# Attention and a two-layer MLP on one core: weight sums moved from GpSimd to VectorE, activation tables fetched by tiny activations, scores and sums rescheduled

## The chip, the cores and the metric

The kernel runs on one core of a Trainium2 chip. The metric is device time in microseconds (us), median over runs. TensorE (PE) multiplies, VectorE (DVE), ScalarE (ACT) and GpSimd (POOL) do the rest, and the DMA engines, 16 on the profile's page, move data. Every time in this text comes from a timed run or from the profile of one execution. Such an execution is some 2 us shorter in its span than in its time, as the span runs from the first to the last of the program's own instructions. An execution is called slow here when its time is more than 1.5% above the fastest of the same kernel, and fast otherwise; ratios are of fast runs alone.

## The reference

```python
# q, k, v: (8 batches, 8 heads, 576 tokens, 64)
q_c, k_c, v_c = (t.reshape(B, H, 9, 64, 64) for t in (q, k, v))      # chunks of 64 tokens
scores = q_c @ k_c.transpose(0, 1, 2, 4, 3) / sqrt(64)
attn = softmax(scores)                                               # within a chunk
x = (attn @ v_c) -> (4608 tokens, 512)                               # heads side by side
h = x @ w_in                                                         # 512 x 2048
g = h * sigmoid(beta * h)
out = g @ w_out                                                      # 2048 x 512
```

## The kernel before

The 4608 tokens are nine blocks of 512 (0 to 8). A block goes through layer 1 (`h`, Silu) and layer 2 (`out`), while the attention of a later block is fitted in between: transposes of q and k on VectorE (`T_items`), scores on PE and exponentials on ScalarE (`emit_sc`), the attention product on PE and its norm on VectorE (`emit_pv`), and a transposing DMA into `xt`. Blocks 1 to 8 use a Strassen-Winograd scheme with seven products in place of eight. It needs sums of weights (`sw`, and `tw` for layer 2), of activations (`xs`) and of Silu outputs (`s1` to `s4`). In the traces an engine's instructions come in the order in which the program emits them: in the changed kernel the last copy to `xt` starts at 56.63 us, behind the table load of 55.23 to 56.51 that is emitted ahead of it.

The weight sums of layer 2, four operations of 128 x 2048 elements:

```python
    def emit_tw(n):
        ...
        o, a_, b_ = {1: (t1, b12, b11), 2: (t2, b22, t1), 3: (t3, b22, b12), 4: (t4, b21, t2)}[n]
        nc.gpsimd.tensor_tensor(out=o, in0=a_, in1=b_, op=ALU.subtract)
```

Half of layer 1 (`unit`; `prod` is four matmuls, `snap` a copy from PSUM on VectorE, a spacer is one plain tile of layer 1, and more):

```python
        prod("A", a11, b11, True)
        snap("u1", "A")
        prod("B", a12, b21, True)
        nc.vector.tensor_tensor(out=c1[:, :, up_], in0=bank["B"], in1=sb["u1"], op=ALU.add)
        spacers[0]()
        prod("A", swr[1], ts[1], False)       # the first one to need xs, and u1 copied
        ...
        for i in range(2):
            silu(m2 + i, up_, bank["A"][:, i])
        for i in range(2):
            silu(m2 + i, dn_, sb["t"][:, i])
        for i in range(2):
            silu(m1 + i, slice(0, BLK), c1[:, i])
```

Norm and transpose of one attention product (`x16` comes from a pool of three buffers):

```python
            nc.vector.reciprocal(out=rr, in_=xx[:, :, :, D:D + 1])
            nc.vector.tensor_tensor(out=yy, in0=src, in1=rr.to_broadcast(shape), op=ALU.mult)
        ...
            nc.sync.dma_start_transpose(out=xt_t[j][:, :, t0:t0 + 128], in_=xf)
```

Layer 2 of block j, from block 2 on (`mm` are the seven products of 16 matmuls, `pv` is the attention product with its norm, `fill` holds eight sums `s1` and `s2`):

```python
            mm[0](); emit_sum(j, 3, 1); emit_sum(j, 3, 3)
            pv(0)
            dve(4)                      # four of the sums
            mm[1](); cB(); pv(1)
            while fill: dve()           # the other four
            mm[2](); pv(2)
            mm[3](); pv(3); sc(0)
            emit_sum(j, 4, 0); emit_sum(j, 4, 1)
            mm[4](); emit_sum(j, 4, 2); emit_sum(j, 4, 3); cD()
            mm[5](); cC(); sc(1); emit_xs(na); mm[6]()
```

Block 1 computes four groups of scores (for blocks 2 and 3) and from there on the kernel is one block ahead.

The softmax here doesn't subtract the row's maximum and nothing guards it: scores larger than these inputs give would overflow.

## Time and profile before

| | before |
|---|---|
| time | 321.67 us median of 3 runs (320.79 to 321.75) |
| span of the profiled run | 318.4 us |
| PE busy | 274.9 us, 86% |
| mean granted clock of PE | 0.984 |

From the page of the kernel before, the PE line of the busy times and the line of the clock, in tenths for 40 slices of the span (PEld is TensorE's loading of weights, x the number of instructions):

```profile
PE 274.9 (86%) x3520; PEld 191.0 (60%) x3520; DVE 227.8 (72%) x411; ACT 159.2 (50%) x270; POOL 119.4 (38%) x114
PEclk9999999789989999999999999999999999999999
```

PE is the engine to keep busy; two places show a lower clock. The timeline tells where PE stood idle. Its columns are start and duration in us, engine, line, operation, tiles written and read, number of instructions, and in brackets the idle time before and what ended it. Four stretches of PE in the kernel before:

```profile
54.32 1.03 PE L244 MATMUL hps<-xt,wi 128*128 128x512 f16 x4
62.19 1.01 PE L297 MATMUL wA<-xs,sw 128*128 128x256 f16 x4 [6.84 <-DVE u L305]
...
89.36 0.45 PE L158 MATMUL sc<-qT,kT 32*64 32x64 f16 x32 [0.47 <-DVE kT L130]
93.62 0.32 PE L158 MATMUL sc<-qT,kT 32*64 32x64 f16 x8 [3.81 <-DVE kT L130]
...
209.70 0.28 PE L397 MATMUL oA<-w_out,gt 128*128 128x256 f16 x1 [0.67 <-ACT gt L308]
210.31 1.38 PE L397 MATMUL oA<-w_out,gt 128*128 128x256 f16 x11 [0.33 <-ACT gt L308]
...
219.39 0.32 PE L186 MATMUL x<-vb,et 64*64 64x65 f16 x16 [1.21 <-DVE x L203]
```

The first pair is the start of block 1: the product that needs `u1` copied and `xs` waits 6.84 us for VectorE. The second is layer 2 of block 1: scores wait 3.81 us for a key transpose. The last three lines are from block 5 and return in other blocks: 1.0 us at the start of layer 2 for Silus, and 1.21 us in front of the fourth attention product for the norm of the third.

Why VectorE is late at 55 us: its timeline and that of GpSimd, in the kernel before.

```profile
44.69 3.13 DVE L121 TENSOR_SCALAR w_out<-w_out,binv 128x512 f16<-128x512 f16 x4 [2.58 <-DMA w_out<-in_moe_w_out_dram]
...
54.27 2.42 DVE L277 TENSOR_TENSOR xs<-xt 128x512 f16<-128x512 f16 x1 [0.17 <-ACT xt L223]
56.72 4.15 DVE L278 TENSOR_TENSOR xs<-xt,xs 128x512 f16<-128x512 f16 x1
60.79 0.41 DVE L279 TENSOR_TENSOR xs<-xt 128x512 f16<-128x512 f16 x1
```

```profile
48.19 8.22 POOL L369 TENSOR_TENSOR tw<-w_out,tw 128x2048 f16<-128x2048 f16 x2
56.35 4.24 POOL L369 TENSOR_TENSOR tw<-w_out 128x2048 f16<-128x2048 f16 x1
```

Operations of the same shape take 0.41 us or 2.42 and 4.15 us; the two long ones end at 56.69 and 60.87, and GpSimd's sums end at 56.41 and 60.59.

The clock around the two holes, from the view of stretches (from:to, length, then per engine the busy time and the number of instructions in the order PE, PEld, DVE, ACT, POOL, then the granted clock, the DMA share and GB/s):

```profile
62.20:64.00 1.80, 1.80 (x9) 1.31 (x9) 1.38 (x2) 0.00 (x0) 0.00 (x0) 0.50 0.00 0
64.00:66.00 2.00, 2.00 (x9) 0.82 (x8) 1.85 (x2) 0.20 (x1) 0.00 (x0) 0.56 0.04 8
...
93.60:97.00 3.40, 3.38 (x26) 2.52 (x27) 0.00 (x0) 1.08 (x2) 0.00 (x0) 0.57 0.00 0
```

The clock was 0.50 from 58.95 to 65.78 us and from 93.08 to 96.50, that is until 3.6 us after the end of the first hole and 2.9 us after that of the second. In the first stretch four matmuls of 128x512 took 1.91 us (from 63.85), and just behind it 1.03 (from 66.11), so these two holes cost more than their length.

One more line, from VectorE's timeline of block 2: the last norm of a block waits for a DMA.

```profile
125.87 0.69 DVE L203 TENSOR_TENSOR x<-x,rd 128x512 f16<-128x512 f32 x1 [0.56 <-DMA xt<-x]
```

Its `x16` buffer is that of the first norm of the block (three buffers), whose transposing DMA was issued at 118.33 and had landed only at 125.78. The median on the page for such transposes is 3.0 us, and one in block 5, where no q and k batch is loaded, took 2.4 (213.01 to 215.41). In between ran the loads of a q and a k batch, issued at 115.60 and 116.33, landed at 121.08 and 125.33. In blocks 3 and 4 the first transpose landed 0.4 us after the load of k as well (157.27 after 156.82, 188.90 after 188.48).

### The profile page before, as it was taken

The page shows a single profiled execution, that of the slowest core. Times are in us where ns is not written, and L with a number is a line of the kernel's source. Part 1 is how long each engine was busy: PE and PEld are TensorE (multiplying, and loading weights), DVE is VectorE, ACT ScalarE, POOL GpSimd, SP SyncE. Part 2 cuts the span into 40 slices and gives each one's busy share as a digit, 9 for nine tenths or more (in the row PEclk, how much of TensorE's full clock was granted, in tenths as well). Part 3 has the DMA queues.
Part 4 walks back from the last instruction along what each step waited for, and adds up shares of the span by engine and source line. Part 5 has one row for each costly group of instructions (what it writes and reads, how often), then busy time and mean ns, then how long its engine had stood idle before and what let it go on. Part 6 is the DMA issues. An engine that isn't in the chain of part 4 may idle for free.

```text
span 318.4 us, 8248 instructions
## 1 busy us (share of the span) xinstructions
PE 274.9 (86%) x3520; PEld 191.0 (60%) x3520; DVE 227.8 (72%) x411; ACT 159.2 (50%) x270; POOL 119.4 (38%) x114
## 2 busy tenths in 40 slices
PE   2889988198949988998899889988998899889894
PEld 0464444155836656766675667666766676676583
DVE  3673467977875878787878786878756775686574
ACT  1268244267423852585257535753584458415820
POOL 8633299616104261346133614341443113213400
PEclk9999999789989999999999999999999999999999
DMA  7999999600933939393949393904390430152002
GB/s 116 179 208 212 187 210 200 173 2 6 191 90 73 70 45 190 106 87 51 184 115 77 56 182 115 74 19 85 103 73 19 84 101 1 30 83 90 2 33 99
DMA packets 69588, 31.99 MB, mean 100 GB/s; under 512 B 53680, under 2 KB 63920, under 8 KB 69552
## 3 DMA queue, kind: packets, MB, share of 16 engines
q0 software_dynamic: 44960, 18.35, 47.9%
q1 hardware_dynamic: 24448, 12.99, 17.4%
q8 instruction: 27, 0.44, 0.6%
q10 hardware_dynamic: 144, 0.13, 0.1%
q14 instruction: 9, 0.07, 0.1%
HBM read 36.71 MB, written 9.44 MB: 145 GB/s over the span
## 4 chain that ended last, share of the span: by engine, by line
PE 43%; DVE 29%; DMA 12%; ACT 9%; issue 5%; POOL 1%; DVEq 0%; ACTq 0%; POOLq 0%
PE oA L397 12%; PE hps L244 11%; DMA w_out<-in_moe_w_out_dram 10%; ACT gt L308 7%; PE wA L297 6%; DVE x L203 5%; DVE s L357 5%; PE wX L297 5%; PE oC L397 4%; DVE s L355 3%; DVE kT L130 3%; PE sc L158 3%; DVE qT L130 2%; DMA ku<-in_k_dram 2%; DVE osb L416 2%
## 5 line engine op out<-in xcount | busy, mean ns | idle before, releaser
L244 PE MATMUL hps<-xt,wi 128*128 128x512 f16 (+1 forms) x336 | 81.2, 372 | 0.8 <-ACT xt L223 0.7
L254 ACT ACTIVATE gt<-hps,beta 128x512 f16<-128x512 f32 x80 | 52.6, 684 | 25.9 <-PE hps L244 25.7
L397 PEld LDWEIGHTS <-s 128*128 128x128 f16 x496 | 47.5, 99 | 7.0 <-DVE s L361 0.3
L244 PEld LDWEIGHTS <-wi 128*128 128x128 f16 x336 | 33.0, 98 | 23.8 <-issue 1.6
L397 PEld LDWEIGHTS <-gt 128*128 128x128 f16 x384 | 35.8, 98 | 16.1 <-ACT gt L308 10.2
L305 DVE COPY u<-wA 128x512 f32<-128x512 f32 x48 | 33.0, 688 | 16.7 <-PE wA L297 16.7
L397 PE MATMUL oA<-tw,s 128*128 128x256 f16 x368 | 44.1, 273 | 0.0
L328 POOL TENSOR_TENSOR t<-u,w 128x512 f32<-128x512 f32 x16 | 20.6, 1285 | 55.8 <-PE hps L244 36.5
L297 PEld LDWEIGHTS <-sw 128*128 128x128 f16 x256 | 25.4, 99 | 19.4 <-issue 9.8
L408 ACT COPY u<-oA 128x512 f32<-128x512 f32 x24 | 14.1, 588 | 43.5 <-PE oA L397 43.5
L466 POOL TENSOR_TENSOR o<-t,o 128x512 f32<-128x512 f32 x7 | 8.9, 1267 | 66.6 <-ACT o L463 66.6
L98 POOL DMA_DIRECT2D vb<-in_v_dram x32 | 27.4, 875 | 10.1 <-DMA wi<-in_moe_w_in_dram 6.3
L167 ACT ACTIVATE et<-sc 128x512 f16<-128x512 f32 x34 | 18.5, 594 | 24.6 <-PE sc L158 24.4
L297 PE MATMUL wA<-xs,sw 128*128 128x256 f16 x128 | 19.7, 278 | 6.8 <-DVE u L305 6.8
L203 DVE TENSOR_TENSOR x<-x,rd 128x512 f16<-128x512 f32 x34 | 23.5, 691 | 2.7 <-DMA xt<-x 1.7
L435 POOL TENSOR_TENSOR w<-u,u 128x512 f32<-128x512 f32 x7 | 10.2, 1458 | 39.6 <-ACT u L408 34.2
L297 PEld LDWEIGHTS <-wi 128*128 128x128 f16 x192 | 18.7, 98 | 9.8 <-issue 4.4
L130 DVE STREAM_TRANSPOSE qT<-qu 128x576 f32<-128x576 f32 x16 | 20.0, 1250 | 5.7 <-DMA qu<-in_q_dram 5.5
L158 PE MATMUL sc<-qT,kT 32*64 32x64 f16 x1088 | 14.1, 196 | 11.4 <-DVE kT L130 11.1
L397 PE MATMUL oA<-w_out,gt 128*128 128x256 f16 x128 | 17.7, 274 | 7.0 <-ACT gt L308 7.0
L167 ACT ACT_TABLE_LOAD x7 | 9.0, 1283 | 28.8 <-PE sc L158 28.8
L158 PEld LDWEIGHTS <-kT 32*64 32x64 f16 x1152 | 12.2, 111 | 16.3 <-DVE kT L130 12.5
(83 smaller groups left out, 444.2 us busy)
## 6 DMA issues: line engine op xcount, KB each, us to landing
out_dram<-osb SPq DMA_DIRECT2D x21, 256.0 KB, 2.7
vb<-in_v_dram POOLq DMA_DIRECT2D x32, 144.0 KB, 5.5
qu<-in_q_dram POOLq DMA_DIRECT2D x7, 576.0 KB, 6.5
ku<-in_k_dram POOLq DMA_DIRECT2D x7, 576.0 KB, 10.0
out_dram<-o SPq DMA_DIRECT2D x14, 256.0 KB, 2.2
wi<-in_moe_w_in_dram POOLq DMA_DIRECT2D x4, 512.0 KB, 12.5
w_out<-in_moe_w_out_dram POOLq DMA_DIRECT2D x4, 512.0 KB, 16.8
qu<-in_q_dram POOLq DMA_DIRECT2D x2, 288.0 KB, 5.4
```

The costliest lines, as they stand in the source:

```text
L98: nc.gpsimd.dma_start(out=t[64 * hp:64 * hp + 64, 2 * z:2 * z + 2, :, 0:D].rearrange("p s c d -> p (s c) d"), in_=v[b, h0:h0 + 2].rearrang ...
L130: nc.vector.transpose(out=dst[b][:, z].rearrange("p t r e -> p (t r e)").bitcast(FP32).rearrange("p (t r) -> p r t", r=RUN), in_=src[b][:, ...
L158: nc.tensor.matmul(out=sc[a % 2][o0:o0 + 64, z, c, :], lhsT=kk[:, cb * CH:(cb + 1) * CH, e], rhs=qq[:, cb * CH:(cb + 1) * CH, e], start=(e ...
L167: nc.scalar.activation(out=et, in_=sc[s], func=ACTF.Exp, scale=scale)
L203: nc.vector.tensor_tensor(out=yy, in0=src, in1=rr.to_broadcast(shape), op=ALU.mult,)
L244: nc.tensor.matmul(out=hps_t[j, m][:, c0:c1], lhsT=w_r[m // 4][:, 2 * z + e, m // 2 % 2, m % 2, :], rhs=xt_t[j][:, n, c0:c1], start=(n == ...
L254: nc.scalar.activation(out=gt_t[j][:, m, :], in_=hps, func=ACTF.Silu, scale=beta2[:, m % 2, m // 2:m // 2 + 1],)
L297: nc.tensor.matmul(out=bank[b][:, i, :], lhsT=a[:, kk, q, i, :], rhs=rhs[:, kk, :], start=(first and i == 0 and kk == 0), stop=(kk == 1), ...
L305: nc.vector.tensor_copy(out=sb[nm], in_=bank[b])
L308: nc.scalar.activation(out=gt_t[j][:, m, cols], in_=src, func=ACTF.Silu, scale=beta2[:, m % 2, m // 2:m // 2 + 1],)
L328: nc.gpsimd.tensor_tensor(out=sb["t"], in0=sb["u3"], in1=sb["w1"], op=ALU.add)
L397: nc.tensor.matmul(out=bank[name][:, i, :], lhsT=a[:, kk, i * 128:(i + 1) * 128], rhs=b[:, kk, :], start=(first and i == 0 and n == 0), st ...
```

## The change

The intent: take GpSimd's sums out of VectorE's way, keep table loads off the waits, let block 1 do less, and put each norm ahead of sums that are not yet needed. The core of the diff (cut where marked):

```diff
@@ Silus of layer 1 (unit)
         for i in range(2):
+            silu(m1 + i, slice(0, BLK), c1[:, i])
+        for i in range(2):
             silu(m2 + i, dn_, sb["t"][:, i])
-        for i in range(2):
-            silu(m1 + i, slice(0, BLK), c1[:, i])
@@ weight sums of layer 2
-        nc.gpsimd.tensor_tensor(out=o, in0=a_, in1=b_, op=ALU.subtract)
+        nc.vector.tensor_tensor(out=o, in0=a_, in1=b_, op=ALU.subtract)
@@ block 0
         scale_w_out(3)
         load_v(2)
+        load_qk(3)
         emit_tw(1)
-        load_qk(3)
         emit_tw(2)
-        emit_tw(4)
-        emit_tw(3)
@@ before block 1
+        def table(func):
+            nc.scalar.activation(out=warm2, in_=warm, func=func, scale=1.0)   # 128x1
+        table(ACTF.Silu)
...
+        emit_xp(7)
+        emit_xs(1)
+        emit_tw(4)
+        emit_tw(3)
@@ blocks: which batch of q and k is transposed in layer 1, and where scores go
+            if j == 1:
+                order = (2, 2, 2, 2)
+            elif j == 2:
+                order = (3, 3, 4, 4)
+            else:
+                order = (j + 2,) * 4
...
+            late = j <= 2          # before: j == 1, which then did four groups of scores
+            if late:
+                hooks[KFF] = lambda: [table(ACTF.Exp), emit_sc(2 * na)]
@@ layer 2 (not late)
             dve(4)
             mm[1]()
-            cB()
             pv(1)
-            while fill:
-                dve()
+            cB()
+            dve(2)
             mm[2]()
             pv(2)
+            dve(2)
             mm[3]()
             pv(3)
+            table(ACTF.Exp)
             sc(0)
-            emit_sum(j, 4, 0), (j, 4, 1) here, (j, 4, 2), (j, 4, 3) behind mm[4]
+            for p in range(4):
+                emit_sum(j, 4, p)
+            if j == 2:
+                T(4, 2)
             mm[4]()
...
+            if j == 1:
+                T(3, 2)
             emit_xs(na)
             mm[6]()
+            table(ACTF.Silu)
```

In blocks 1 and 2 ("late") each attention product stands one matmul group later, and a group of scores stands in front of layer 2. Block 1 now does two groups of scores, block 2 four.

More of the change, by code (lines that the diff above doesn't have):

```diff
@@ L68 @@
     warm = const.tile([128, 1], FP32)
+    warm2 = const.tile([128, 1], FP32)
     zero = const.tile([128, BLK], FP16)
@@ L561 @@
         nc.vector.memset(warm, 0.0)
-        nc.scalar.activation(out=warm, in_=warm, func=ACTF.Exp, scale=1.0)
+        nc.scalar.activation(out=warm2, in_=warm, func=ACTF.Exp, scale=1.0)
         for g4 in range(4):
@@ L633, with T @@
             f()
+        def table(func):
+            nc.scalar.activation(out=warm2, in_=warm, func=func, scale=1.0)
+        table(ACTF.Silu)
+        TQ = {b: T_items(b) for b in range(2, B)}
+        def T(b, n=1):
+            for _ in range(n):
+                if TQ.get(b):
+                    TQ[b].pop(0)()
+        emit_xp(7)
+        emit_xs(1)
+        emit_tw(4)
+        emit_tw(3)
         for j in range(1, NB):
             na = j + 1
-            hooks = {}
-            tr = T_items(j + 2) if j + 2 < B else []
             if j == 1:
-                T2 = T_items(2)
-                hooks = {9: T2[0], 11: T2[1], 13: T2[2], 15: T2[3], KFF: lambda: emit_sc(4)}
-                emit_xp(7)
-                emit_xs(1)
-            elif tr:
-                hooks = {10: tr.pop(0), 11: tr.pop(0), 14: tr.pop(0), 15: tr.pop(0)}
+                order = (2, 2, 2, 2)
[3 more added lines that the diff above has]
+                order = (j + 2,) * 4
+            hooks = {m: (lambda b=b: T(b)) for m, b in zip((10, 11, 14, 15), order)}
+            late = j <= 2
+            if late:
+                hooks[KFF] = lambda: [table(ACTF.Exp), emit_sc(2 * na)]
             L1(j, hooks)
@@ L652, in sc @@
             def sc(n):
-                if na + 1 < NB:
+                if na + 1 < NB and j > 1:
                     emit_sc(2 * na + 2 + n)
-            def go(lst):
-                if lst:
-                    lst.pop(0)()
-            if j + 3 < B and j + 3 > 3:
+            if j > 1 and j + 3 < B or j == 1:
                 load_qk(j + 3)
@@ L665 @@
             emit_sum(j, 3, 3)
-            if j > 1:
+            if not late:
                 pv(0)
@@ L669 @@
             mm[1]()
-            cB()
-            if j == 1:
+            if late:
                 pv(0)
-                emit_sc(5)
+                emit_sc(2 * na + 1)
             else:
                 pv(1)
-            while fill:
-                dve()
+            cB()
+            dve(2)
             mm[2]()
-            if j == 1:
-                pv(1)
-            else:
-                pv(2)
-            go(tr)
-            mm[3]()
-            if j == 1:
-                pv(2)
-            else:
-                pv(3)
-            if j > 1:
-                sc(0)
-            emit_sum(j, 4, 0)
-            emit_sum(j, 4, 1)
-            go(tr)
-            mm[4]()
-            emit_sum(j, 4, 2)
-            emit_sum(j, 4, 3)
-            cD()
-            if j == 1:
-                pv(3)
-            go(tr)
-            go(tr)
-            if j == 1:
+            pv(1 if late else 2)
+            dve(2)
+            mm[3]()
+            pv(2 if late else 3)
+            if not late:
+                table(ACTF.Exp)
+                sc(0)
+            for p in range(4):
+                emit_sum(j, 4, p)
+            if j == 2:
+                T(4, 2)
+            mm[4]()
+            cD()
+            if late:
+                pv(3)
                 sc(0)
@@ L706 @@
                 cC()
-            if j > 1:
+            if not late:
                 sc(1)
+            if j == 1:
+                T(3, 2)
             if na < NB:
@@ L711 @@
             mm[6]()
-            if j == 1:
+            if late:
                 sc(1)
+            table(ACTF.Silu)
             if j + 2 < B:
```

## The prediction

> **What bounds the kernel now.** TensorE, with holes. The page gives PE 86% busy over 318.4 us, nearly always at full clock. In the timeline a steady block (131.75 to 163.30) takes 31.55 us, PE busy 29.0. The holes, from the PE timeline:
> - Start of block 1: 6.84 us (55.4 to 62.2) waiting for the first copy `u`. VectorE is late because two differences `xs` take 2.42 and 4.15 us, in later blocks 0.42. GpSimd runs the weight sums `tw` (4.1 us each) then. [...]each long `xs` ends as a `tw` ends. The clock is then 0.50 to 0.56 until 66.
> - Second half of block 1 (77.7 to 100.2, steady: 18.0): scores wait 3.8 us for key transposes, the clock falls to 0.57, the next block waits 0.8 us for an exponential.
> - Every block: 0.67+0.33 us at the start of layer 2 for the Silus of `c`; 1.2 us before the fourth attention product, whose norm is queued behind four sums.
>
> **What the change does (us).**
> 1. `tw` to VectorE: an estimate from 418 ns (512 columns) and 691 (1024) gives 1.24 each. Two stand before block 1's norms, two after `xs`. The last weight scaling loses its contention (3.13 to about 1.5). A Silu table load (1.28) now precedes the last `xt` copy, delaying it about 1. The first `u` comes near 60 instead of 61.5: the hole shrinks to some 4, half of the clock loss probably goes. Gain 3.
> 2. Block 1 loses two score groups and the wait for transposes: gain 5.5.
> 3. Block 2 gets four score groups and two more transposes (2.5) ahead of its last norm, which lands about 3 later (a DMA transpose takes 3.0 to land), so `xs` and the first `u` of block 3 are late. Loss 3.
> 4. Norm before sums: removes the 1.2 hole in blocks 5, 6, 7. In 3 and 4 the last norm already waits for the first DMA transpose, which lands when the q/k load has landed (125.3). That date does not move; the stall should move to the product that needs the `s4` sums. Gain 0.2 each.
> 5. Silu order: estimated 0.4 of the 1.0, real in blocks 5 to 8. With 4: 1.5 each in 5 to 7, total 4.5; block 8 0.4, and its tail 0.7, as `s4` no longer stands behind the last combination.
> 6. Dummy activations: table loads off the waits for scores and layer 1, but PE does not wait there: 0. Four more loads (1283 ns each), in idle ScalarE time.
>
> Sum: -3 -5.5 +3 -0.4 -4.5 -1.1 = -11.5.
>
> **Prediction:** 310 us, 80% range 304 to 315.5. Chances: faster by over 2% 0.87, within 2% 0.11, slower 0.02.
>
> **What would show it.** 1: all `xs` at 0.42, `tw` near 1.24 on VectorE, first PE hole 3 to 5. 2: no wait of scores over 1 in block 1, second half 17 to 19. 3: PE holes of 2 to 4 at the start of block 3, behind DMA and `xs`. 4: blocks 5 to 7 near 29.9, 3 and 4 near 31.3 with a wait of `oC` for `s4`. 5: wait for Silu about 0.5. 6: 20 table loads.
>
> **What would make it wrong.** The transposes of step 3 hidden better, or the DMA landing earlier (then 305); the clock falling again in block 1[...].

The sum came to -11.5 us, from 321.67 to about 310.

## The result, and the profile after

| | before | after |
|---|---|---|
| time, median | 321.6 us (4 runs, 320.79 to 321.75) | 309.44 us (4 runs, 309.19 to 311.57) |
| ratio of the fast runs | | 0.9644, 95% interval 0.9609 to 0.9680 |
| span of the profiled run | 318.4 us | 309.8 us (its time: 311.57) |
| PE busy | 86% | 89% |

A ratio is the mean time of one kernel's fast runs over that of the other's of the same rounds, so it is not quite the ratio of the medians. The profiled run of the changed kernel happens to be its slowest; a second trace, of an execution of 309.78 us, comes from the first experiment.

The page of the changed kernel:

```profile
PE 276.0 (89%) x3520; PEld 190.4 (61%) x3520; DVE 225.1 (73%) x415; ACT 168.8 (54%) x291; POOL 101.7 (33%) x110
PEclk9999997869997999999999999999999999999999
```

In these two executions there is more low clock than before, not less (mean 0.977 against 0.984); over the runs of experiment 1's call the two kernels do not differ in this (0.977 to 0.989 changed, 0.973 to 0.984 before). PE's timeline of the changed kernel, at the places of the lines before (the line numbers are one higher):

```profile
49.53 0.32 PE L187 MATMUL x<-vb,et 64*64 64x65 f16 x16 [2.17 <-DVE x L204]
...
57.25 1.02 PE L245 MATMUL hps<-xt,wi 128*128 128x512 f16 x4 [0.67 <-ACT xt L224]
61.71 1.01 PE L298 MATMUL wA<-xs,sw 128*128 128x256 f16 x4 [3.44 <-DVE u L306]
...
96.21 0.60 PE L298 MATMUL wA<-xs,sw 128*128 128x256 f16 x4 [2.26 <-DVE u L306]
...
156.92 0.39 PE L398 MATMUL oC<-w_out,s 128*128 128x256 f16 x2 [1.04 <-DVE s L362]
...
207.46 0.28 PE L398 MATMUL oA<-w_out,gt 128*128 128x256 f16 x1 [0.24 <-ACT gt L309]
208.07 1.37 PE L398 MATMUL oA<-w_out,gt 128*128 128x256 f16 x11 [0.33 <-ACT gt L309]
```

The hole at the start of block 1 is 3.44 us instead of 6.84, but 2.17 and 0.67 us ahead of it are new. Block 2 has a new hole of 2.26 us; VectorE's timeline in front of it shows the two transposes that the change puts last in block 1 (`T(3, 2)`), 2.3 us of work ahead of `xs`:

```profile
91.14 1.25 DVE L131 STREAM_TRANSPOSE qT<-qu 128x576 f32<-128x576 f32 x1
92.23 1.24 DVE L131 STREAM_TRANSPOSE kT<-ku 128x576 f32<-128x576 f32 x1
93.31 1.11 DVE L278 TENSOR_TENSOR xs<-xt 128x512 f16<-128x512 f16 x1
```

In block 5 the wait for the Silu of `c` is 0.24 instead of 0.67 us, and there is no wait in front of the fourth attention product. In block 3 (the line at 156.92), and likewise in block 4, `oC` now waits for the `s4` sums.

VectorE and ScalarE of the changed kernel at the start of block 1:

```profile
44.93 1.31 DVE L122 TENSOR_SCALAR w_out<-w_out,binv 128x512 f16<-128x512 f16 x4 [2.56 <-DMA w_out<-in_moe_w_out_dram]
46.17 1.21 DVE L370 TENSOR_TENSOR tw<-w_out 128x2048 f16<-128x2048 f16 x1
...
57.23 0.43 DVE L278 TENSOR_TENSOR xs<-xt 128x512 f16<-128x512 f16 x1 [1.05 <-ACT xt L224]
57.69 0.42 DVE L279 TENSOR_TENSOR xs<-xt,xs 128x512 f16<-128x512 f16 x1
```

```profile
55.23 1.28 ACT L635 ACT_TABLE_LOAD   x1
56.52 0.20 ACT L635 ACTIVATE warm<-warm 128x1 f32<-128x1 f32 x1
56.63 0.57 ACT L224 COPY xt<-xps 128x512 f16<-128x512 f16 x1
```

All `xs` of block 1 take 0.42 us, the scaling of `w_out` 1.31 instead of 3.13, a weight sum 1.21 to 1.23 instead of 4.1. But `xs` starts 1.05 us after VectorE was free: the last copy to `xt` stands behind the table load of the dummy activation. One long `xs` is left, that of 1.11 us in block 2 shown above: it ends at 94.42, 0.28 us after an addition on GpSimd (92.87 to 94.14).

The clock in the changed kernel:

```profile
61.70:64.00 2.30, 2.29 (x10) 1.46 (x10) 1.77 (x3) 0.00 (x0) 0.00 (x0) 0.50 0.05 16
64.00:66.00 2.00, 2.00 (x9) 0.97 (x7) 0.31 (x1) 0.68 (x1) 0.00 (x0) 0.50 0.00 0
...
98.00:100.00 2.00, 2.00 (x8) 1.01 (x7) 0.33 (x1) 0.69 (x1) 0.00 (x0) 0.50 2.35 156
```

Where the time came from, by the starts of PE's instructions in the timelines of two fast executions, before (span 318.4) and the second one of the changed kernel (span 308.0). "First use of u" is the `wA<-xs,sw` that follows the hole; "layer 1" runs from there to the first `oA<-w_out,gt`, "layer 2" from there to the next block's first use of u:

| stretch | before | changed | difference |
|---|---|---|---|
| to the first use of u in block 1 | 62.19 | 60.01 | -2.18 |
| block 1, layer 1 | 15.52 | 15.55 | +0.03 |
| block 1, layer 2 | 24.23 | 18.77 | -5.46 |
| block 2, layer 1 | 11.83 | 14.52 | +2.69 |
| block 2, layer 2 | 19.72 | 20.69 | +0.97 |
| block 3, layer 1 | 11.83 | 12.55 | +0.72 |
| blocks 3 and 4, layer 2 | 39.45 | 39.09 | -0.36 |
| blocks 5, 6, 7, layer 2 | 57.71 | 52.11 | -5.60 |
| block 8, layer 2 to the end | 17.87 | 16.71 | -1.16 |

The rest (layer 1 of blocks 4 to 8) differs by 0.02 us at most in each. The sum is 10.4 us, the difference of the spans. "Layer 2" of block 1 holds two effects in this table: from its first `oA<-w_out,gt` to the first matmul of block 2 it took 14.56 us instead of 22.49 (-7.9), and from there to the first use of u 4.20 instead of 1.73 (+2.5).

### The profile page after: what moved, and what is told of

It is laid out like the page before. It is cut to its first block, busy times and chain, and to the rows that moved or that the text cites. A ratio compares the mean times of both kernels' runs of the same rounds, so it can differ in the third digit from the quotient of the medians.

```text
span 309.8 us, 8218 instructions
## 1 busy us (share of the span) xinstructions
PE 276.0 (89%) x3520; PEld 190.4 (61%) x3520; DVE 225.1 (73%) x415; ACT 168.8 (54%) x291; POOL 101.7 (33%) x110
## 4 chain that ended last, share of the span: by engine, by line
PE 45%; DVE 24%; DMA 19%; ACT 6%; issue 5%; POOL 1%; DVEq 0%; ACTq 0%; POOLq 0%
PE oA L398 11%; PE hps L245 11%; DMA w_out<-in_moe_w_out_dram 10%; PE wA L298 6%; DMA xt<-x 6%; PE wX L298 5%; DVE qT L131 4%; ACT gt L309 3%; PE oB L398 3%; DVE kT L131 3%; DVE c L333 3%; PE oC L398 3%; DMA vb<-in_v_dram 3%; DVE s L362 2%; PE oD L398 2%
## 5 line engine op out<-in xcount | busy, mean ns | idle before, releaser
L245 PE MATMUL hps<-xt,wi 128*128 128x512 f16 (+1 forms) x336 | 83.0, 378 | 1.4 <-ACT xt L224 1.3
L398 PEld LDWEIGHTS <-s 128*128 128x128 f16 x496 | 46.3, 98 | 10.6 <-DVE s L362 4.7
L168 ACT ACTIVATE et<-sc 128x512 f16<-128x512 f32 x34 | 18.4, 593 | 28.1 <-PE sc L159 28.1
L99 POOL DMA_DIRECT2D vb<-in_v_dram x32 | 27.4, 876 | 10.1 <-DMA wi<-in_moe_w_in_dram 6.3
L298 PE MATMUL wA<-xs,sw 128*128 128x256 f16 x128 | 20.5, 286 | 6.9 <-DVE u L306 6.9
L309 ACT ACTIVATE gt<-c,beta 128x512 f16<-128x512 f32 x32 | 21.4, 715 | 4.0 <-DVE c L333 4.0
L131 DVE STREAM_TRANSPOSE kT<-ku 128x576 f32<-128x576 f32 x16 | 20.0, 1248 | 2.3 <-DMA ku<-in_k_dram 2.3
L436 POOL TENSOR_TENSOR w<-u,u 128x512 f32<-128x512 f32 x7 | 8.8, 1262 | 38.0 <-ACT u L409 38.0
```

Of the source, the lines that this page charges most:

```text
L99: nc.gpsimd.dma_start(out=t[64 * hp:64 * hp + 64, 2 * z:2 * z + 2, :, 0:D].rearrange("p s c d -> p (s c) d"), in_=v[b, h0:h0 + 2].rearrang ...
L131: nc.vector.transpose(out=dst[b][:, z].rearrange("p t r e -> p (t r e)").bitcast(FP32).rearrange("p (t r) -> p r t", r=RUN), in_=src[b][:, ...
L168: nc.scalar.activation(out=et, in_=sc[s], func=ACTF.Exp, scale=scale)
L245: nc.tensor.matmul(out=hps_t[j, m][:, c0:c1], lhsT=w_r[m // 4][:, 2 * z + e, m // 2 % 2, m % 2, :], rhs=xt_t[j][:, n, c0:c1], start=(n == ...
L298: nc.tensor.matmul(out=bank[b][:, i, :], lhsT=a[:, kk, q, i, :], rhs=rhs[:, kk, :], start=(first and i == 0 and kk == 0), stop=(kk == 1), ...
L309: nc.scalar.activation(out=gt_t[j][:, m, cols], in_=src, func=ACTF.Silu, scale=beta2[:, m % 2, m // 2:m // 2 + 1],)
```

## The experiments

My theory was that of the prediction, item by item: operations of VectorE that take longer beside sums on GpSimd (2.42 and 4.15 instead of 0.41 us) at the start of block 1, transposes in block 1, norms behind sums in blocks 5 to 7, a DMA in 3 and 4, Silus, and nothing from the dummies. The rivals are named in each expectation. Twelve kernels ran, each with five timed rounds, on four chips. The kernel before took 320.83, 321.17, 321.35 and 321.26 us (median of 11 runs each; one, 459.16 us at a mean clock of 0.567, was slow).

### 1. The changed kernel again

> The changed kernel once more, unaltered, for a second trace. The profiled run of it took 311.57 us where its other runs took 309.2 to 309.8, and its clock fell to 0.50 at the start of block 2 (96 to 101). Theory: that fall is not of the change but of that run[...]; then this trace shows the first half of block 2 at 11.8 us instead of 14.5 and a span near 307.5. Rival: the hole of 2.3 us always costs the clock; then the trace shows 0.5 there again and the same 14.5 us.

Measured: 310.68 us (309.08 to 311.81), ratio 0.9677. The clock fell again in block 2, and its layer 1 took 14.52 us: my theory fell, the rival holds. The hole there, 2.26 us in the first trace and so shorter than one step of the clock's record (its times lie 3.41 us apart), was followed by half clock both times. What differs between the two executions is the clock in block 0 (the first has a fall behind its hole of 2.17 us, the second none behind 2.04).

### 2. Four buffers for the normed tile

```diff
-    x_p = ctx.enter_context(tc.tile_pool(name="x", bufs=3))
+    x_p = ctx.enter_context(tc.tile_pool(name="x", bufs=4))
```

> The changed kernel with four instead of three buffers for the normed attention tile. Theory: in blocks 3 and 4 the last norm can't start before the first DMA transpose has left the shared buffer, which the q/k load delays to 7.6 us after its issue; the s4 sums and then oC wait behind that norm (1.32 and 1.55 us in the two blocks). With a fourth buffer that wait goes: the oC wait falls to about 0.3, blocks 3 and 4 go from 33.3 and 31.4 to about 32 and 30, and the whole falls by 2 to 3 us (to 306.5 to 307.5). Rival: the sums are late because VectorE's queue or GpSimd's subtraction is in the way; then the wait of oC stays near 1.3 and the time at 309.4.

Measured: 308.29 us, ratio 0.9590 against 0.9677 on the same chip. The norm and sums of block 3 in VectorE's timeline, first of the changed kernel, then with four buffers:

```profile
153.76 0.20 DVE L202 RECIPROCAL rd<-x 128x8 f32<-128x8 f32 x1
155.84 0.69 DVE L204 TENSOR_TENSOR x<-x,rd 128x512 f16<-128x512 f32 x1 [1.87 <-DMA xt<-x]
156.44 1.42 DVE L362 TENSOR_TENSOR s<-gt,s 128x512 f16<-128x512 f16 x4
```

```profile
153.74 0.20 DVE L202 RECIPROCAL rd<-x 128x8 f32<-128x8 f32 x1
153.98 0.69 DVE L204 TENSOR_TENSOR x<-x,rd 128x512 f16<-128x512 f32 x1
154.59 1.42 DVE L362 TENSOR_TENSOR s<-gt,s 128x512 f16<-128x512 f16 x4
```

The wait of 1.87 us is gone, the sums come 1.85 us earlier, `oC` waits for nothing, and blocks 3 and 4 (first matmul to first matmul) take 31.61 and 29.79 us instead of 33.42 and 31.41; block 5 gives 0.45 of it back (29.97 instead of 29.52). The fall of 2.4 us is within the 2 to 3 expected. So the gain of the new order was indeed caught in blocks 3 and 4 by a buffer that a DMA held (in block 3 of the changed kernel from 148.12 to 155.75 us).

### 3. The weight sums back on GpSimd

```diff
-        nc.vector.tensor_tensor(out=o, in0=a_, in1=b_, op=ALU.subtract)
+        nc.gpsimd.tensor_tensor(out=o, in0=a_, in1=b_, op=ALU.subtract)
```

> The changed kernel with the four weight sums back on GpSimd, in the changed order. Theory[...]: the sums take 4.1 us each again, the last scaling of w_out is stretched to about 3 us, and some xs take 1.5 to 4 us instead of 0.42, as each waits for a sum to end; the first u of block 1 comes near 60.5 to 61.5, about as in the kernel before or as in the changed one, so 309.5 to 311. Rival: the long xs of the kernel before came from the order (sums not yet done, DMA writes), not from the engine; then all xs stay at 0.42 and block 1 starts 2 to 4 us earlier than in the changed kernel, as VectorE has 4.9 us less to do.

Measured: 314.29 us, ratio 0.9785, so 3.6 us slower than the changed kernel on that chip. VectorE and GpSimd:

```profile
44.72 5.47 DVE L122 TENSOR_SCALAR w_out<-w_out,binv 128x512 f16<-128x512 f16 x4 [2.38 <-DMA w_out<-in_moe_w_out_dram]
...
59.25 3.56 DVE L278 TENSOR_TENSOR xs<-xt 128x512 f16<-128x512 f16 x1 [1.05 <-ACT xt L224]
62.85 0.42 DVE L279 TENSOR_TENSOR xs<-xt,xs 128x512 f16<-128x512 f16 x1
```

```profile
45.97 4.06 POOL L370 TENSOR_TENSOR tw<-w_out 128x2048 f16<-128x2048 f16 x1
...
58.48 4.05 POOL L370 TENSOR_TENSOR tw<-w_out 128x2048 f16<-128x2048 f16 x1
```

The long `xs` is back and ends 0.3 us after a sum ends; the rival is refuted. My size was off (309.5 to 311 expected) because the scaling was stretched to 5.47 us, not to 3: in this order a sum runs beside most of the scaling (45.97 to 50.03). Not all of the 3.6 us is this: the same execution also shows half clock for 6.83 us in block 0, and a block 4 that is 2.0 us longer, with a transposing DMA that landed 8.3 us after its issue. Both kinds of operation are longer beside a sum on GpSimd, the difference `xs` with 3.56 instead of 0.42 us and the four scalings with 5.47 instead of 1.31; why they are is not shown.

### 4. Without the dummy activations

```diff
         def table(func):
-            nc.scalar.activation(out=warm2, in_=warm, func=func, scale=1.0)
+            pass
```

> The changed kernel without the dummy activations; the table loads then stand in front of the first real activation that needs them. Theory: nothing on TensorE waits for those loads in blocks 3 to 8 (0 there), and at the start of block 1 the dummy's load delays the last xt copy by 1.1 us, so without it the first u comes up to 1.1 us earlier; 308.2 to 309.6. Rival: the dummies hide 1.28 us twice a block; without them the time rises by 1 us or more per block, to 315 or above.

Measured: 308.32 us (307.53 to 309.15), ratio 0.9608 against 0.9677: **faster** without them, by 2.4 us. The trace shows no wait of PE for a table anywhere. At the start of block 1 the last `xt` copy no longer waits for a table, so the wait of 0.67 us for `xt` is gone and the first use of u comes 5.30 us after the block's first matmul instead of 6.18. And the clock did not fall there: layer 1 of block 1 took 13.69 us instead of 15.55. PE at the start of block 1:

```profile
59.59 0.60 PE L298 MATMUL wA<-xs,sw 128*128 128x256 f16 x4 [3.40 <-DVE u L306]
```

The hole is as long as in the changed kernel (3.40 and 3.44). How the idle time lay here is told in the section on the clock; why it cost no clock is not shown. But this execution, the fastest of the five, is no measure of the others: its mean clock was 0.994, which is by its size about one step of 3.41 us at half clock, while the other four had 0.983 to 0.989, about two or three such steps where the changed kernel has two to four, and still took 308.31 to 309.15 us. So the earlier first use of u (0.88 us) is shown; how the rest of the 2.4 us divides is not, and as all dummies were removed at once, it is not shown that all of it comes from the first one.

### 5. The norms alone, on the kernel before

The edit, condensed to what it does from block 2 on:

```diff
             mm[1]()
-            cB(); pv(1)
-            while fill: dve()
-            mm[2](); pv(2)
+            pv(1); cB()
+            dve(2)
+            mm[2](); pv(2)
+            dve(2)
```

> The kernel before with one part of the change alone: from block 2 on, each norm goes ahead of the later sums. Theory: the 1.2 us hole in front of the fourth attention product goes in all of blocks 2 to 7, but only 5, 6 and 7 keep the gain (1.2 to 1.6 us each); in 2, 3 and 4 it turns into a wait of oC for the s4 sums, because the last norm still waits for the first DMA transpose (gain 0.2 each). Together 4 to 5.5 us of the kernel before's time: a ratio near 0.985. Rival: the hole was worth its 1.2 us in every block; then 2, 3 and 4 shorten as 5 to 7 do, and the ratio is near 0.975.

Measured: 315.32 us, ratio 0.9837 (0.9806 to 0.9867). Blocks 2, 3 and 4 changed by +0.25 (in block 2 the load of k landed at 125.66 instead of 125.33 us, and the transpose that the last norm waits for at 126.11 instead of 125.78), -0.15 and -0.36 us, blocks 5, 6 and 7 by -1.55, -1.59 and -1.13. In block 3 the wait of `oC` is the new one:

```profile
158.67 0.39 PE L397 MATMUL oC<-w_out,s 128*128 128x256 f16 x2 [0.81 <-DVE s L361]
```

The theory holds, the rival (a gain in every block) falls.

### 6. The Silu order alone, on the kernel before

```diff
         for i in range(2):
+            silu(m1 + i, slice(0, BLK), c1[:, i])
+        for i in range(2):
             silu(m2 + i, dn_, sb["t"][:, i])
-        for i in range(2):
-            silu(m1 + i, slice(0, BLK), c1[:, i])
```

> The kernel before with one part of the change alone: the Silus of c ahead of those of t. Theory: the two waits at the start of layer 2 go from 0.67 and 0.33 to 0.24 and 0.33 (the first Silu of c then waits for its sum on VectorE), so 0.43 us in each of blocks 2 to 8, 3 us together, ratio 0.990 to 0.992; block 1 has scores there and gains nothing. Rival: something else in the block takes it back (the third sum now waits for the Silus of t); then the blocks keep 31.5 us and the ratio is 0.998 or more.

Measured: 319.69 us, ratio 0.9963 (0.9941 to 0.9985). By the profile, blocks 2 to 8 became shorter by 0.21 to 0.45 us each, 2.4 us together, near what was expected; but block 1, which the edit does not touch in layer 2, was 0.86 us longer in that execution. The timed gain is 1.2 us with an interval from 0.5 to 1.9. So the step is seen in the blocks, and less than half of the 3 us in the time. Of the 0.86 us, 0.41 lie in layer 1 of block 1, where the low clock ended 4.6 us after the first use of u instead of 3.6; and in experiment 5, whose edit leaves block 1 alone, that block was 0.71 us longer too. So block 1 differs by this much between executions; whether that is all of the missing gain was not settled.

### 7. The scores of block 3 back in block 1

```diff
-            late = j <= 2
+            late = j == 1           # and all four transposes T(3) and four groups of scores in block 1
```

> The changed kernel with the scores of block 3 back in block 1, with all key and query transposes of that batch, as the kernel before had them. Theory: in the second half of block 1 scores wait for transposes 3 us or more again and the clock halves after it; that half takes 19 to 22 us instead of 14.6, and the hole of 2.3 us at the start of block 2 is replaced by the wait for an exponential (0.8), with block 2 shorter by 4 to 6 us; net 1 to 4 us slower than the changed kernel. Rival: the waits only moved to block 2; then the time is that of the changed kernel within 1 us.

Measured: 314.42 us, ratio 0.9808 against 0.9644 and 0.9677 of the changed kernel (other chips), so 4 to 5 us slower. Layer 1 start to layer 1 start, block 1 took 46.40 us instead of 36.30, block 2 31.34 instead of 36.32, block 3 31.54 instead of 33.42. PE waited twice for a transpose:

```profile
91.60 0.64 PE L159 MATMUL sc<-qT,kT 32*64 32x64 f16 x32 [1.87 <-DVE kT L131]
95.20 0.32 PE L159 MATMUL sc<-qT,kT 32*64 32x64 f16 x8 [2.96 <-DVE kT L131]
```

Two expectations were missed on the same side: the second half of block 1 took 24.1 us, not 19 to 22, with the clock at half for two steps (6.83 us) instead of one, and the whole lost a little more than 1 to 4 us. So moving this work pays, though of the 10.1 us that block 1 gains 6.9 are given back in blocks 2 and 3.

### 8. Zeros in the holes

```diff
                 emit_m(j, m)
+                if m == 8 and j <= 2:
+                    emit_idle(12 if j == 1 else 8)      # matmuls of zeros that nobody reads
```

> The changed kernel with matmuls of zeros that nobody reads put into its two largest holes: 12 of them while TensorE waits for the first u of block 1 (hole 3.44 us), 8 in block 2 (2.26 us). They change no wait of the kernel's own work. Theory: [...]without that idle time it stays at 1.0, the layer 1 after the first u goes from 15.5 to about 13.7 us in block 1 and from 14.5 to 12.6 in block 2, and the whole is 3 to 4 us faster than the changed kernel, near 306.5. Rival: those 2 us are waits on VectorE and ScalarE in a block that starts late; then the two stretches stay at 15.5 and 14.5 and the time does not fall.

> The experiment with matmuls of zeros in the two holes once more, on the kernel with four buffers for the normed tile, because the profiled execution of the first one was in the slow state with a late DMA in block 4. Theory: as before, the clock is 1.0 in blocks 1 and 2, their layers 1 take 13.7 and 12.6 us from the first use of u on, and the whole is 3 to 4 us under the 308.3 us of the four-buffer kernel: ratio to the kernel before 0.947 to 0.951. Rival: no gain from the clock; ratio 0.959.

The "it" that stays at 1.0 is the granted clock of PE.

Measured: 309.17 us (305.78 to 313.29), ratio 0.9593; on the four-buffer kernel 308.35 us (306.76 to 311.95), ratio 0.9607 (0.9571 to 0.9644). The two stretches did what was expected in both traces: 13.68 and 12.61 us, and 13.68 and 12.60, with a clock of 1.0. As the changed kernel has 15.55 and 14.52, the clock's part is 1.9 us in each. But the whole gained some 2 us in the first and nothing in the second, where the ratio of the four-buffer kernel was 0.9590. Both profiled executions were slow and show late DMA transposes around blocks 3 and 4 (in block 4 of the first the last norm waited 3.54 us for one), so their later blocks explain nothing about the fast runs. The zeros also did not leave the other waits alone, as the expectation had it: in both traces the first use of u came later in block 2 (4.58 and 4.93 us after the block's start instead of 4.20) and in block 3 (4.82 and 4.67 instead of 3.09). The clock's part is seen in its own stretches; that the whole gains 4 us by it is not shown, and what took them back in the fast runs of the second kernel is open. Three of the four fast runs of the first took 308.14 to 310.13 us although their mean clock was 0.988 to 0.994; only the fourth, at 0.999, took 305.78.

### 9. A new version, and its parts

The version moves the weight sums to where VectorE has nothing to do, and takes the dummies out (condensed):

```diff
-    x_p = ... bufs=3
+    x_p = ... bufs=4
@@ emit_tw
-        nc.vector.tensor_tensor(...)
+        (nc.gpsimd if n == 3 else nc.vector).tensor_tensor(...)
@@ block 0
+        emit_tw(1)
         scale_w_out(3)
         load_v(2)
         load_qk(3)
-        emit_tw(1)
-        emit_tw(2)
+        emit_tw(3)
...
         emit_xs(1)
-        emit_tw(4)
-        emit_tw(3)
@@ table(): pass
@@ layer 2
             mm[0]()
+            if j == 1:
+                emit_tw(2)
...
             dve(4)
+            if j == 1:
+                emit_tw(4)
+            elif j == 2:
+                T(4)
...
-            if j == 2: T(4, 2)      mm[4]()   cD()   pv(3)
+            mm[4]()   pv(3)   if j == 2: T(4, 2)   cD()
...
-                T(3, 2)             # order of block 2 is (3, 3, 4, 4)
+                T(3)                # order of block 2 is (3, 3, 3, 4)
```

> A new version on the changed kernel: no dummies, four buffers for the normed tile, the first weight sum ahead of the last scaling of w_out, the third on GpSimd before any activation difference runs, the second and fourth in layer 2 of block 1 where VectorE waits for an attention product, one of block 1's two transposes moved into block 2, and block 2's last norm ahead of its last two transposes. Theory: [...]the clock stays at 1.0; with the oC waits gone, 299 to 303 us. Rival: the moved operations find no gap on VectorE and stretch block 1's layer 2 by as much as they save; 305 to 308.

That the clock stays at 1.0 was an estimate of mine, from shorter holes at the start of blocks 1 and 2.

Measured: **296.1 us** (295.57 to 297.1), ratio 0.9229 (0.9205 to 0.9253), correct. The theory's range was 299 to 303, so it was too cautious. The clock and the two first uses of u:

```profile
PE 270.4 (92%) x3520; PEld 188.7 (64%) x3520; DVE 225.3 (76%) x414; ACT 160.7 (54%) x270; POOL 106.4 (36%) x111
PEclk9999999999999999999999999999999999999999
```

```profile
55.03 0.60 PE L298 MATMUL wA<-xs,sw 128*128 128x256 f16 x4 [1.13 <-DVE u L306]
...
86.87 0.60 PE L298 MATMUL wA<-xs,sw 128*128 128x256 f16 x4 [1.79 <-DVE u L306]
```

The mean granted clock of that execution is 1.000, and the span 294.8 us. PE's busy time is 5.6 us less than in the profile of the changed kernel for the same 3520 matmuls. In that profile PE was busy for 11.9 us in the three stretches at half clock, and half of that, some 6 us, is my estimate of what the full clock saves.

Two more runs take it apart. First the places of the weight sums alone, with dummies and three buffers:

> The changed kernel with only the weight sums placed anew (first ahead of the last scaling of w_out, third on GpSimd before any xs, second and fourth in layer 2 of block 1); dummies and three buffers kept. Theory: the hole of 2.0 us in block 0 goes, the one at the start of block 1 shrinks from 3.44 to about 2.2, the hole in block 2 grows by up to 0.5; 4 to 6 us faster than the changed kernel, 304 to 306. Rival: layer 2 of block 1 stretches by the 2.4 us of sums put there; 308 or more.

Measured: 302.97 us, ratio 0.9440 (0.9399 to 0.9481), better than expected. The hole in block 0 is gone, the first use of u in block 1 comes at 55.16 us instead of 60.01, and layer 2 of block 1 did not grow (14.56 us from its first matmul to the next block's, changed kernel 14.57): VectorE really had room there. In the profiled run the clock still fell once in block 1 and once in block 2. The six runs of this kernel form two groups, which is the plainest sign of what the clock costs: three at a mean clock of 0.998 or 0.999 took 301.51 to 301.79 us, three at 0.981 to 0.989 took 304.16 to 305.04.

Then the dummies put back into the new version:

> The new version (296.1 us) with the dummy activations put back as the changed kernel has them. Theory: the first Silu dummy delays the last xt copy of block 1 by about 1.1 us, which lengthens the hole from 1.13 to about 2.2 us and may halve the clock; elsewhere nothing: 297 to 299.5. Rival: the dummies cost nothing there[...] or even help; 295.5 to 296.5.

Measured: 299.34 us, ratio 0.9320 (0.9290 to 0.9350) against 0.9229 (another chip), so about 2.9 us slower. The first use of u in block 1 comes 3.90 us after the block's first matmul instead of 3.03. In the profiled run the clock fell in block 2 (layer 1 14.57 us instead of 12.92), and a late DMA transpose held up block 5 by 1.3 us. But the clock is not the whole cost of the dummies: three of the six runs had a mean clock of 1.000 and took 298.19 to 298.68 us, where the new version at 1.000 took 296.1 to 297.1. The 0.9 us at the start of block 1 are seen; the rest was not traced. The fourth buffer and the moved transposes of block 2 were not run alone in the new version.

### Where the clock was halved

The records of the clock in each trace change on a grid of 3.41 us, whose place differs from execution to execution (by 1.03 us between the two traces below). Two traces serve as the measure, that of the kernel before and the first one of the changed kernel. These are their falls, with the time in which PE ran no matmul in the step of 3.41 us just ahead of each:

| trace | clock 0.50, from and to | PE idle in the step ahead |
|---|---|---|
| before | 58.95 to 65.78 us | 3.41 us |
| before | 93.08 to 96.50 us | 3.28 us |
| changed | 49.74 to 53.15 us | 2.16 us |
| changed | 59.98 to 66.81 us | 2.38 us |
| changed | 97.53 to 100.94 us | 2.29 us |

In the same two traces 15 other steps at full clock held 0.92 to 1.55 us of idle time, and the clock was full at the end of each. Left out are the steps ahead of the record's first entry (14.58 and 12.19 us) and those at the end of the program, where PE has no work left (3.41 and 2.79 us, both followed by half clock). Matmul ends are modelled in the profile, so the idle times are known to a few tenths only. Each fall lasts one step or two.

The length of a single hole does not tell the two cases apart. In the trace of experiment 4 the hole of 3.40 us lay across two steps, with 1.80 and 1.79 us of idle time in them, and the clock did not fall. In the changed kernel the additional wait of 0.67 us for the last `xt` copy and the first part of the hole of 3.44 us lay in one step, the one with 2.38 us, and it fell; so it did in all four traces that begin block 1 that way (both of the changed kernel, the four-buffer one and that of experiment 7). That it is so in every execution is not shown, and the mean clocks of the other runs of experiment 4 speak against it.

## Why the prediction was right

The time, 309.44 us, lies 0.6 us from the forecast of 310, and most items hold one by one; the second set of runs gave 310.68. Several errors cancelled.

| item of the prediction | predicted, us | measured in traces, us |
|---|---|---|
| 1. weight sums to VectorE, with the clock | -3 | -2.2 |
| 2. block 1 relieved | -5.5 | -5.5 (-7.9 in its second half, +2.5 in the start of block 2) |
| 3. block 2 loaded, block 3 late | +3 | +4.4 (0.97 + 2.69 + 0.72) |
| 4. and 5. norms and Silus, blocks 5 to 7 | -4.5 | -5.6 |
| 4. blocks 3 and 4 | -0.4 | -0.4 |
| 5. block 8 with its tail | -1.1 | -1.2 |
| 6. dummies | 0 | cost 2.4 (timed, experiment 4; 0.9 of it in the trace, inside item 1) |

- **Item 1.** That `xs` is long where it runs beside a sum on GpSimd is shown by experiment 3 (3.56 us, against 0.42 without), and the hole shrank to 3.44 us as forecast ("some 4"). The half of the clock loss that was to go did not go: layer 1 of block 1 stayed at 15.5 us. The step that failed was the estimate of the clock, for which I took the length of a single hole; in the changed kernel it stood behind a wait of 0.67 us, and the two left PE idle for 2.38 us in the step ahead of the fall. I also had the first two sums too cheap: they stand ahead of the norm of an attention product and opened a new hole of 2.0 to 2.2 us in block 0, which is gone where they stand elsewhere (experiment 9).
- **Item 2.** The sum holds to 0.1 us, but by two errors that cancel. The second half of block 1 took 14.6 us, below the 17 to 19 announced, so 7.9 us were gained and not 5.5. The prediction had not seen that two transposes of batch 3, put right ahead of the `xs` of block 2, would open a hole of 2.26 us there, with 2.5 us lost. Experiment 7 shows from the other side that the move pays, and that the hole belongs to it.
- **Item 3.** The net was close, but the parts were not as I told them. The first use of u in block 3 came 1.4 us late (3.09 instead of 1.74 us after the block's start), less than the "2 to 4" announced. The last transposed tile landed 2.7 us later, near the forecast of 3 (18.4 us after the start of layer 2 instead of 15.7); but in the kernel before it had landed 2.3 us ahead of block 3 (129.43 against 131.75), and this reserve took up part of the delay. What I missed is the clock: behind the 2.26 us hole at the start of block 2 it was 0.50 for 3.41 us. Of the 2.7 us that layer 1 of block 2 lost, this is 1.9: with the clock at 1.0 it still took 12.6 us instead of 11.83 (experiment 8).
- **Item 4.** Blocks 5 to 7 gained 2.0, 2.0 and 1.6 us where 1.5 each was forecast. In block 5 this is 0.43 from the Silus and 1.21 from the named hole, 0.19 that the third attention product had also waited (its place in the timeline, 2.04 us after the product ahead of it against 1.85), and 0.10 in the scores behind it. The capture by the DMA in blocks 3 and 4, the least obvious item, is shown by experiments 2 and 5.
- **Item 5** is seen in each block (0.67 to 0.24), as estimated. Its timed effect alone was 1.2 us of the 3 expected.
- **Item 6** was wrong in sign. The delay of 1.1 us was in the prediction, but within item 1 and without its effect on the clock. The tables were not on PE's way before, so fetching them early could gain nothing, and the first fetch took a place in ScalarE's order where it was on the way (0.9 us). The rest of the 2.4 us is not traced to a place.

The range (304 to 315.5) was wide enough for these errors; that they nearly cancelled (in item 2 the hole against the larger gain, and 1.9 us lost to the clock in block 2 against more gain in blocks 5 to 7) is luck.

## What to carry to other kernels

Count what an added instruction delays in its engine's order, not whether the engine is idle on average: a 1.28 us table fetch in front of a copy made the first use of u 0.9 us later, two transposes ahead of a small sum opened a hole of 2.26 us, and the same weight sums, put where VectorE waited for PE anyway, gave 7 us more than the change had. Look at the clock behind a hole of the matmul engine and not at the hole's length alone: here a hole of 3.44 us was followed by half clock and one of 3.40 was not, and the layer behind it took 15.55 and 13.69 us. When a reorder helps some blocks and not others, look for what is held from outside, here a buffer behind a DMA; one more buffer set it free.
